# A decayed linear attention that feeds a SwiGLU block: half steps of the third tile ahead of the first outputs, and loads of group 7 ahead of a transpose

## The chip, the cores and the metric

The kernel runs on one core of a Trainium2 chip. The metric is the device time of one execution in microseconds. A core has five engines that run their own instruction streams: TensorE (PE in the profile; PEld is its weight load), VectorE (DVE), ScalarE (ACT), GpSimd (POOL) and SyncE (SP). [...] Transfers between HBM and the core's memory are issued by SP and ACT here and run on the core's 16 DMA engines.

## The reference

Inputs are q, k and v of shape (batch 4, heads 8, sequence 768, head size 64), one decay per head, lam, and three weight matrices. The first part is causal linear attention with decay, worked in blocks of 64 positions:

```
for b in range(nb):
    intra = einsum('bhic,bhjc->bhij', qb, kb) * Dmask     # lam ** (i - j), lower triangle
    intra = einsum('bhij,bhjd->bhid', intra, vb)
    inter = einsum('bhid,bhde->bhie', qb * lam_pow, kv_state)
    out[block] = intra + inter
    kv_state = lam_block * kv_state + einsum('bhsd,bhse->bhde', kb * rev_pow, vb)
```

Its result, laid out as 3072 tokens of 512 numbers, is x of the second part:

```
g = x @ w_gate                     # 512 -> 1536
silu = g * (1 / (1 + exp(-g)))
out = (silu * (x @ w_val)) @ w_out # 1536 -> 512
```

## The kernel before

**Groups and tiles.** The kernel works the sequence in blocks of 128. A group is one batch and two such blocks; there are 12 groups, 0 to 11. Two groups make a tile of 512 tokens (four blocks b of 128), so there are six tiles t, 0 to 5. Attention goes group by group, the SwiGLU block tile by tile. A tile has 12 steps fc, one for each 128 columns of the 1536. ffn_gate (L508) runs four matmuls over the input rows (L514) and Silu on ACT (L518); ffn_val (L520) runs four more (L528) and multiplies on DVE into h (L531). A full step is 512 columns wide. A half step takes two of the four blocks and is 256 wide: blocks 0 and 1 need only the attention of the tile's first group, blocks 2 and 3 only that of the second. ffn_out (L538) makes the output of one block: twelve matmuls over h and w_out (L547), a copy on ACT (L549) and a DMA that ACT issues (L550). The very last output is made in two halves of 256 columns, the second copied by DVE and sent by SP.

**A group of attention.** Its k, q and v are loaded by SP (load_fp32, L93; from group 6 on each of k and q in four DMAs, L106, v in two). cast_scaled (L255) casts k on ACT (L258) and scales q on DVE (L260) and then issues a DMA transpose on SP (L251); groups 0 to 2 are transposed on TensorE instead (pe_transpose, L289). v_scale (L235) makes v_s from v on POOL (L238). upd_mm (L366, matmuls L382) multiplies k by v_s for the running state, upd_copy (L390) copies that out on ACT (L404), and state (L410) adds it up on POOL (L421 to L432). scores (L308, matmuls L326, from group 6 on L352) multiplies q by k; the causal mask is put on by DVE later, by run_later (L333, L357). core_a (L490) multiplies q by the state (L461), core_b (L495) multiplies the masked scores by v_s (L474), and evac (L481) casts the result to xt, the input of the SwiGLU block (L486). Two helpers bundle these: ahead(g) does upd and scores; attend(g) does core_a of g, then upd_mm, upd_copy and scores of g + 1, then core_b of g and state of g + 1.

**What sets the order.** Each engine runs its instructions in the order in which the program issues them. The order is written by hand: lines 574 to 665 are a fixed start (groups 0 and 1 and the first steps), and then a list of steps with a plan of calls that follow each step (at, L675; the loop of L766 issues a step and then its calls). Tile 1 is done in 24 half steps, s1a and s1b. Behind the last of them come, in one row, the four outputs of tile 0 with the attention of group 5, the cast, transpose and v_s of group 6 and the loads of group 7 between them (L736 to L746). Tile 2 follows in twelve full steps, with ahead(6) after step 2, cast_scaled of groups 7 and 8 after steps 3 and 7, attend(6) after step 6, attend(7) after step 10, and the outputs of tile 1 after steps 0, 3, 7 and 9.

**Queues and buffers.** SP's queue carries all loads and all DMA transposes in program order; ACT's carries the outputs. PSUM is used as a ring of eight banks. w_out comes in six pieces that are cast by wo_cast, five on POOL and one on ACT. h has two tiles of 12 columns blocks each. At the very start, before any data is there, TensorE runs matmuls on constants (warm_up, L127), and in between them the matmul that spreads lam over the partitions (L163).

Of the kernel before, what the change touches and what calls it, by code (L numbers as in the profile page):

```python
# [37 lines left out]
def _body(ctx, tc, nc, q, k, v, lam, moe_w_gate, moe_w_val, moe_w_out, out):  # L38
    B, H, S, D = q.shape
    HP = H // 2  # L40
    BLK = 128
# [4 lines left out]
    FC = DFF // 128  # L46
    NG = NBLK * B // 2
# [22 lines left out]
    h_pool = ctx.enter_context(tc.tile_pool(name="h", bufs=2))  # L70
# [90 lines left out]
    lam_ps = bank()  # L161
    warm_up(4)
    nc.tensor.matmul(lam_ps[:, 0:H], ones[:, 0:128], lam_row, start=True, stop=True)  # L163
    warm_up(3)
# [355 lines left out]
    def ffn_val(t, fc, b0=0, b1=B):  # L520
        if ("h", t) not in st:
            st[("h", t)] = h_pool.tile([128, FC, B, BLK], BF16, name="h", tag="h")
        h_sb, xt, sil = st[("h", t)], st[("xt", t)], st[("sil", t, fc, b0)]
        N = (b1 - b0) * BLK
        fs = slice(fc * 128, fc * 128 + 128)
        vp = bank()
        for mc in range(MC):
            nc.tensor.matmul(vp[:, 0:N], wv_sb[:, mc, fs],  # L528
                             xt[:, b0 // 2:b1 // 2, mc].rearrange("p g b n -> p g (b n)"),
                             start=(mc == 0), stop=(mc == MC - 1))  # L530
        nc.vector.tensor_tensor(out=h_sb[:, fc, b0:b1].rearrange("p b n -> p (b n)"),  # L531
                                in0=sil[:, 0:N], in1=vp[:, 0:N], op=ALU.mult)
# [5 lines left out]
    def ffn_out(t, b, last=False):  # L538
        h_sb = st[("h", t)]
        osb = osb_pool.tile([128, DM], FP32, name="osb", tag="osb")  # L540
        row = groups[2 * t + b // 2][0] * S + (groups[2 * t + b // 2][1] * 2 + b % 2) * BLK
        halves = ((0, DM // 2, nc.scalar.copy, nc.scalar), (DM // 2, DM, nc.vector.tensor_copy, nc.sync)) \
            if last else ((0, DM, nc.scalar.copy, nc.scalar),)
        for c0, c1, fn, eng in halves:
            ps = bank()[:, 0:c1 - c0]
            for fc in range(FC):
                nc.tensor.matmul(ps, h_sb[:, fc, b], wo_sb[:, fc, c0:c1],  # L547
                                 start=(fc == 0), stop=(fc == FC - 1))
            fn(out=osb[:, c0:c1], in_=ps)  # L549
            eng.dma_start(out=bass.AP(tensor=out.tensor, offset=out.offset + row * DM + c0,  # L550
                                      ap=[[DM, 128], [1, c1 - c0]]),
                          in_=osb[:, c0:c1])
# [104 lines left out]
    w_cast()  # L657
# [29 lines left out]
    at(s0[4], load_group, 2, "v")  # L687
# [8 lines left out]
    at(s0[8], v_scale, 2, nc.gpsimd)  # L696
# [34 lines left out]
    at(s1b[6], v_scale, 5, nc.gpsimd)  # L731
    at(s1b[8], wo_cast)
    at(s1b[9], core_a, 4)
    at(s1b[10], core_b, 4)
    at(s1b[10], wo_cast, ACTC)
    at(s1b[11], ffn_out, 0, 0)  # L736
    at(s1b[11], ahead, 5)
    at(s1b[11], run_later, 3)
    at(s1b[11], ffn_out, 0, 1)
    at(s1b[11], core_a, 5)  # L740
    at(s1b[11], ffn_out, 0, 2)
    at(s1b[11], core_b, 5)
    at(s1b[11], cast_scaled, 6)
    at(s1b[11], load_group, 7)
    at(s1b[11], v_scale, 6, nc.gpsimd)
    at(s1b[11], ffn_out, 0, 3)  # L746

    outs = [(1, b) for b in range(4)]
    for t in range(2, NG // 2):
        sn = [step(t, fc) for fc in range(FC)]  # L750
        if t == 2:
            at(sn[2], ahead, 6)
        for j, g in ((3 if t == 2 else 0, 2 * t + 3), (7 if t == 2 else 6, 2 * t + 4)):
            if g < NG:
# [3 lines left out]
                at(sn[1 + j], v_scale, g, nc.gpsimd)  # L758
        if t + 1 < NG // 2:
            at(sn[6 if t == 2 else 4], attend, 2 * t + 2)  # L760
            at(sn[10], attend, 2 * t + 3)
        for n, o in zip((0, 3, 7, 9), outs):
            at(sn[n], ffn_out, *o)
# [42 lines left out]
```

## Time and profile before

| | us |
|---|---|
| runs, median of 4 (lowest to highest) | 228.44 (227.96 to 229.01) |
| the profiled execution's own time | 228.06 |
| its span, first to last instruction | 226.4 |
| busy: PE, PEld | 219.4, 118.5 |
| busy: ACT, DVE, POOL | 107.2, 90.2, 89.6 |

The busy times are shares of one span and engines overlap, so they don't add up. Matmuls are pipelined: a matmul row gives the time from the first start to the modelled end, and the next row can start before it. How long a matmul really takes in a stream is read from where the next one starts: 0.86 for four of 512 columns and 0.44 for four of 256 in the chain of work. The chain is the run of work that ended last, followed back; a wait is put down to what came last before it ended. Lines with a trailing q (SPq, ACTq) are the engine's sequencer issuing a DMA.

### The profile page before, as it was taken

The page shows a single profiled execution, that of the slowest core. Times are in us where ns is not written, and L with a number is a line of the kernel's source. Part 1 is how long each engine was busy: PE and PEld are TensorE (multiplying, and loading weights), DVE is VectorE, ACT ScalarE, POOL GpSimd, SP SyncE. Part 2 cuts the span into 40 slices and gives each one's busy share as a digit, 9 for nine tenths or more (in the row PEclk, how much of TensorE's full clock was granted, in tenths as well). Part 3 has the DMA queues.
Part 4 walks back from the last instruction along what each step waited for, and adds up shares of the span by engine and source line. Part 5 has one row for each costly group of instructions (what it writes and reads, how often), then busy time and mean ns, then how long its engine had stood idle before and what let it go on. Part 6 is the DMA issues. An engine that isn't in the chain of part 4 may idle for free.

```text
span 226.4 us, 5902 instructions
## 1 busy us (share of the span) xinstructions
PE 219.4 (97%) x2443; PEld 118.5 (52%) x2443; DVE 90.2 (40%) x151; ACT 107.2 (47%) x209; POOL 89.6 (40%) x131
## 2 busy tenths in 40 slices
PE   8889999999999999999999999999999999999994
PEld 3666455878864444454544544544544444444443
DVE  2664357685934215545253262253242123222200
ACT  6878584754663536354443453553533423322221
POOL 6676737642894403969262192191150000000000
PEclk9999999999999999999999999999999999999998
DMA  6999999899989487889867749905101101101122
GB/s 198 342 360 382 367 341 315 225 247 373 397 153 213 145 184 193 214 180 230 211 145 191 184 96 229 225 12 139 49 3 48 46 3 46 46 0 46 49 93 93
DMA packets 88012, 39.70 MB, mean 175 GB/s; under 512 B 57650, under 2 KB 83506, under 8 KB 87986
## 3 DMA queue, kind: packets, MB, share of 16 engines
q1 hardware_dynamic: 83474, 32.64, 53.8%
q10 hardware_dynamic: 4512, 6.69, 8.3%
q8 instruction: 19, 0.31, 0.6%
q14 instruction: 7, 0.06, 0.1%
HBM read 28.31 MB, written 6.29 MB: 153 GB/s over the span
## 4 chain that ended last, share of the span: by engine, by line
PE 80%; DMA 8%; POOL 6%; SPq 3%; issue 1%; ACT 0%; DVE 0%; DVEq 0%; POOLq 0%
PE bank L547 27%; PE bank L514 23%; PE bank L528 23%; DMA v<-in_v_dram 5%; DMA wraw<-in_moe_w_val_dram 3%; POOL v_s L238 3%; SPq L99 2%; PE bank L474 2%; PE bank L461 2%; PE bank L382 2%; POOL wo_sb L232 1%; POOL kvf L421 1%; PE bank L352 1%; POOL kvs L424 1%; PE bank L326 1%
## 5 line engine op out<-in xcount | busy, mean ns | idle before, releaser
L531 DVE TENSOR_TENSOR h<-sil,bank 128x512 bf16<-128x512 bf16 (+1 forms) x87 | 51.5, 595 | 108.0 <-PE bank L528 94.1
L514 PE MATMUL bank<-xt,wg_sb 128*128 128x512 bf16 (+1 forms) x348 | 76.6, 343 | 0.0
L528 PE MATMUL bank<-xt,wv_sb 128*128 128x512 bf16 (+1 forms) x348 | 76.4, 342 | 0.0
L518 ACT ACTIVATE sil<-bank 128x512 bf16<-128x512 f32 (+1 forms) x87 | 45.9, 527 | 44.4 <-PE bank L514 41.4
L547 PE MATMUL bank<-wo_sb,h 128*128 128x512 bf16 (+1 forms) x300 | 65.8, 371 | 0.4 <-POOL wo_sb L232 0.4
L528 PEld LDWEIGHTS <-wv_sb 128*128 128x128 bf16 x348 | 34.0, 98 | 28.3 <-POOL wv_sb L221 0.2
L514 PEld LDWEIGHTS <-wg_sb 128*128 128x128 bf16 x348 | 32.4, 98 | 27.2 <-DVE xt L486 0.3
L547 PEld LDWEIGHTS <-h 128*128 128x128 bf16 x300 | 29.1, 98 | 33.0 <-issue 0.7
L549 ACT COPY osb<-bank 128x512 f32<-128x512 f32 (+1 forms) x24 | 13.8, 576 | 53.3 <-PE bank L547 51.3
L238 POOL TENSOR_TENSOR v_s<-v,dec 128x1024 bf16<-128x1024 f32 (+1 forms) x14 | 23.2, 1665 | 11.7 <-DMA v<-in_v_dram 5.9
L421 POOL TENSOR_TENSOR kvf<-kvs,ups 128x256 f32<-128x256 f32 x8 | 5.8, 726 | 46.2 <-ACT ups L404 40.6
L333 DVE TENSOR_TENSOR ssb<-bank,causal 128x512 bf16<-128x512 f32 x24 | 15.3, 684 | 3.6 <-PE bank L326 3.5
L486 ACT CAST xt<-bank 128x512 bf16<-128x512 f32 x21 | 12.8, 667 | 2.9 <-PE bank L474 2.4
L430 POOL CAST kvn<-kvf 64x256 bf16<-64x256 f32 x24 | 12.5, 519 | 1.5
L421 POOL TENSOR_TENSOR kvf<-kvf,ups 128x256 f32<-128x256 f32 x16 | 12.7, 792 | 0.6
L404 ACT COPY ups<-bank 128x256 f32<-128x256 f32 (+1 forms) x24 | 9.5, 449 | 2.5 <-PE bank L382 1.5
L258 ACT CAST qk<-kraw 128x1024 bf16<-128x1024 f32 x9 | 9.4, 1040 | 0.9 <-DMA kraw<-in_k_dram 0.9
L260 DVE TENSOR_TENSOR qk<-qraw,qdn 128x1024 bf16<-128x1024 f32 x6 | 7.9, 1314 | 4.2 <-DMA qraw<-in_q_dram 4.1
L357 DVE TENSOR_TENSOR ssb<-bank,causaln 128x512 bf16<-128x512 f32 x12 | 8.3, 688 | 1.2 <-PE bank L352 1.1
L221 POOL CAST wv_sb<-wraw 128x1024 bf16<-128x1024 f32 (+1 forms) x6 | 5.8, 968 | 5.3 <-DMA wraw<-in_moe_w_val_dram 5.2
L232 POOL CAST wo_sb<-woraw 128x1024 bf16<-128x1024 f32 x5 | 5.8, 1181 | 4.6 <-DMA woraw<-in_moe_w_out_dram 4.6
L474 PE MATMUL bank<-ssb,v_s 64*64 64x128 bf16 (+1 forms) x384 | 6.8, 208 | 0.5 <-ACT guard L445 0.5
(63 smaller groups left out, 118.3 us busy)
## 6 DMA issues: line engine op xcount, KB each, us to landing
out_dram<-osb ACTq DMA_DIRECT2D x23, 256.0 KB, 2.1
v<-in_v_dram SPq DMA_DIRECT2D x16, 256.0 KB, 4.5
woraw<-in_moe_w_out_dram SPq DMA_DIRECT2D x6, 512.0 KB, 7.5
kraw<-in_k_dram SPq DMA_DIRECT2D x24, 128.0 KB, 3.3
qraw<-in_q_dram SPq DMA_DIRECT2D x24, 128.0 KB, 3.5
wraw<-in_moe_w_gate_dram SPq DMA_DIRECT2D x5, 512.0 KB, 7.3
wraw<-in_moe_w_val_dram SPq DMA_DIRECT2D x5, 512.0 KB, 6.9
kraw<-in_k_dram SPq DMA_DIRECT2D x4, 512.0 KB, 6.8
```

Source lines behind the costliest of these rows:

```text
L238: eng.tensor_tensor(out=st[("vs", g)][:, h0:h1], in0=st[("v", g)][:, h0:h1].rearrange("p h (s d) -> p h s d", s=2), in1=vfac(g, h0, h1), o ...
L333: nc.vector.tensor_tensor(out=ssb[:, h2, 2 * c:2 * c + 2].rearrange("p a s n -> p a (s n)"), in0=sp[(c, h2)].rearrange("p (a x) -> p a x", ...
L421: nc.gpsimd.tensor_tensor(out=o, in0=f, in1=u, op=ALU.add)
L430: nc.gpsimd.tensor_copy(out=o[64 - h2 * 64:128 - h2 * 64], in_=f[h2 * 64:h2 * 64 + 64])
L474: nc.tensor.matmul(op[r][h2 * 64:h2 * 64 + 64, cols(g, hp, s)], v_s[ps, 2 * hp + h2, s], ssb[ps, h2, hp * 2 + s] if g >= NAT0 else ssb[ps, ...
L486: fns[r](out=xt[:, g % 2, :, r].rearrange("p h (m s) -> p h s m", s=2) if g < NAT0 else xt[:, g % 2, :, :, r * M:r * M + M], in_=op[r].rea ...
L514: nc.tensor.matmul(gp[:, 0:N], wg_sb[:, mc, fs], xt[:, b0 // 2:b1 // 2, mc].rearrange("p g b n -> p g (b n)"), start=(mc == 0), stop=(mc = ...
L518: nc.scalar.activation(sil[:, 0:N], gp[:, 0:N], AF.Silu)
L528: nc.tensor.matmul(vp[:, 0:N], wv_sb[:, mc, fs], xt[:, b0 // 2:b1 // 2, mc].rearrange("p g b n -> p g (b n)"), start=(mc == 0), stop=(mc = ...
L531: nc.vector.tensor_tensor(out=h_sb[:, fc, b0:b1].rearrange("p b n -> p (b n)"), in0=sil[:, 0:N], in1=vp[:, 0:N], op=ALU.mult)
L547: nc.tensor.matmul(ps, h_sb[:, fc, b], wo_sb[:, fc, c0:c1], start=(fc == 0), stop=(fc == FC - 1))
L549: fn(out=osb[:, c0:c1], in_=ps)
```

## The change

It has these parts.

- **Half steps.** Four half steps of tile 2 (fc 0 to 3, blocks 0 and 1) are put behind tile 1 and ahead of the four outputs of tile 0; in tile 2 itself steps 0 to 3 are then half steps for blocks 2 and 3. h becomes half tiles of six column blocks, five of them instead of two whole ones. group 4's result is cast to xt by DVE and ACT, not by ACT alone.
- **Group 7.** Its k and q are loaded ahead of the first output of tile 0, and so ahead of group 6's transpose on SP; its v behind that transpose. Its v_scale is issued ahead of ahead(6), and so ahead of the state of group 6 on POOL.
- **Order in tile 2.** ahead(6) goes from step 2 to step 4, cast_scaled of groups 7 and 8 from steps 3 and 7 to 4 and 8, attend(6) from step 6 to step 7; the outputs of tile 1 follow steps 1, 5, 7 and 9. v_scale of group 5 goes behind the fifth cast of w_out.
- **Halves for group 2 and for one weight.** v of group 2 is loaded and scaled in two halves, and POOL casts one piece of w_val in two halves.
- **Start and end.** Ahead of lam's matmul stand thirty matmuls of 64 rows and 8 columns, in alternating halves of the rows, and two of 512 columns, instead of four of 512; behind it stand four instead of three. The last output is split into 384 columns (ACT) and 128 (DVE and SP).

```diff
--- before.py
+++ after.py
@@ -44,6 +44,7 @@
     DFF = moe_w_gate.shape[1]
     MC = DM // 128
     FC = DFF // 128
+    FH = FC // 2
     NG = NBLK * B // 2
     M = BLK // 2
 
@@ -67,7 +68,7 @@
     vs_pool = ctx.enter_context(tc.tile_pool(name="vs", bufs=4))
     ssb_pool = ctx.enter_context(tc.tile_pool(name="ssb", bufs=2))
     xt_pool = ctx.enter_context(tc.tile_pool(name="xt", bufs=2))
-    h_pool = ctx.enter_context(tc.tile_pool(name="h", bufs=2))
+    h_pool = ctx.enter_context(tc.tile_pool(name="h", bufs=5))
     sil_pool = ctx.enter_context(tc.tile_pool(name="sil", bufs=3))
     osb_pool = ctx.enter_context(tc.tile_pool(name="osb", bufs=3))
     kv_pool = ctx.enter_context(tc.tile_pool(name="kv", bufs=1))
@@ -159,9 +160,13 @@
            for b in range(B)]
 
     lam_ps = bank()
+    b = bank()
+    for n in range(30):
+        r = slice(n % 2 * 64, n % 2 * 64 + 64)
+        nc.tensor.matmul(b[r, 0:8], warm[r, 0:64], warm[r, 0:8], start=True, stop=True, skip_group_check=True)
+    warm_up(2)
+    nc.tensor.matmul(lam_ps[:, 0:H], ones[:, 0:128], lam_row, start=True, stop=True)
     warm_up(4)
-    nc.tensor.matmul(lam_ps[:, 0:H], ones[:, 0:128], lam_row, start=True, stop=True)
-    warm_up(3)
     def warm_into(b, n, cols=256):
         for _ in range(n):
             nc.tensor.matmul(b[:, 0:cols], warm[:, 0:128], warm[:, 0:cols], start=True, stop=True)
@@ -518,9 +523,10 @@
         nc.scalar.activation(sil[:, 0:N], gp[:, 0:N], AF.Silu)
 
     def ffn_val(t, fc, b0=0, b1=B):
-        if ("h", t) not in st:
-            st[("h", t)] = h_pool.tile([128, FC, B, BLK], BF16, name="h", tag="h")
-        h_sb, xt, sil = st[("h", t)], st[("xt", t)], st[("sil", t, fc, b0)]
+        hn = ("h", t, fc // FH)
+        if hn not in st:
+            st[hn] = h_pool.tile([128, FH, B, BLK], BF16, name="h", tag="h")
+        h_sb, xt, sil = st[hn], st[("xt", t)], st[("sil", t, fc, b0)]
         N = (b1 - b0) * BLK
         fs = slice(fc * 128, fc * 128 + 128)
         vp = bank()
@@ -528,7 +534,7 @@
             nc.tensor.matmul(vp[:, 0:N], wv_sb[:, mc, fs],
                              xt[:, b0 // 2:b1 // 2, mc].rearrange("p g b n -> p g (b n)"),
                              start=(mc == 0), stop=(mc == MC - 1))
-        nc.vector.tensor_tensor(out=h_sb[:, fc, b0:b1].rearrange("p b n -> p (b n)"),
+        nc.vector.tensor_tensor(out=h_sb[:, fc % FH, b0:b1].rearrange("p b n -> p (b n)"),
                                 in0=sil[:, 0:N], in1=vp[:, 0:N], op=ALU.mult)
 
     def ffn_fc(t, fc, b0=0, b1=B):
@@ -536,15 +542,14 @@
         ffn_val(t, fc, b0, b1)
 
     def ffn_out(t, b, last=False):
-        h_sb = st[("h", t)]
         osb = osb_pool.tile([128, DM], FP32, name="osb", tag="osb")
         row = groups[2 * t + b // 2][0] * S + (groups[2 * t + b // 2][1] * 2 + b % 2) * BLK
-        halves = ((0, DM // 2, nc.scalar.copy, nc.scalar), (DM // 2, DM, nc.vector.tensor_copy, nc.sync)) \
+        halves = ((0, DM - 128, nc.scalar.copy, nc.scalar), (DM - 128, DM, nc.vector.tensor_copy, nc.sync)) \
             if last else ((0, DM, nc.scalar.copy, nc.scalar),)
         for c0, c1, fn, eng in halves:
             ps = bank()[:, 0:c1 - c0]
             for fc in range(FC):
-                nc.tensor.matmul(ps, h_sb[:, fc, b], wo_sb[:, fc, c0:c1],
+                nc.tensor.matmul(ps, st[("h", t, fc // FH)][:, fc % FH, b], wo_sb[:, fc, c0:c1],
                                  start=(fc == 0), stop=(fc == FC - 1))
             fn(out=osb[:, c0:c1], in_=ps)
             eng.dma_start(out=bass.AP(tensor=out.tensor, offset=out.offset + row * DM + c0,
@@ -654,7 +659,10 @@
     ffn_gate(0, 1, 0, 2)
     ffn_gate(0, 0, 2, 4)
     w_piece(6, 8)
-    w_cast()
+    w_cast((ACTC,))
+    wv2, wv2r = w_raw.pop(0)
+    for c in range(2):
+        POOLC(out=wv2[:, :, c * 128:c * 128 + 128], in_=wv2r[:, :, c * 128:c * 128 + 128])
     ring[0] = 4
     ffn_val(0, 0, 2, 4)
     ffn_val(0, 1, 0, 2)
@@ -684,7 +692,8 @@
     at(s0[3], swapped_q_table)
     at(s0[4], w_cast)
     at(s0[4], state, 1)
-    at(s0[4], load_group, 2, "v")
+    at(s0[4], load_fp32, 2, nc.sync, v, "v", 0, H // 2)
+    at(s0[4], load_fp32, 2, nc.sync, v, "v", H // 2, H)
     at(s0[5], load_group, 3)
     at(s0[6], w_cast)
     at(s0[7], load_group, 4, "kq")
@@ -693,7 +702,8 @@
     at(s0[8], pe_transpose, 2, 0)
     at(s0[8], pe_transpose, 2, 1)
     at(s0[8], w_cast)
-    at(s0[8], v_scale, 2, nc.gpsimd)
+    at(s0[8], v_scale, 2, nc.gpsimd, 0, H // 2)
+    at(s0[8], v_scale, 2, nc.gpsimd, H // 2, H)
     at(s0[9], scores, 2)
     at(s0[9], run_later, 4)
     at(s0[10], upd_mm, 2)
@@ -728,38 +738,43 @@
     at(s1b[6], run_later, 2)
     at(s1b[6], wo_cast)
     at(s1b[6], wo_cast)
-    at(s1b[6], v_scale, 5, nc.gpsimd)
     at(s1b[8], wo_cast)
+    at(s1b[8], v_scale, 5, nc.gpsimd)
     at(s1b[9], core_a, 4)
-    at(s1b[10], core_b, 4)
+    at(s1b[10], core_b, 4, SPLIT)
     at(s1b[10], wo_cast, ACTC)
-    at(s1b[11], ffn_out, 0, 0)
-    at(s1b[11], ahead, 5)
-    at(s1b[11], run_later, 3)
-    at(s1b[11], ffn_out, 0, 1)
-    at(s1b[11], core_a, 5)
-    at(s1b[11], ffn_out, 0, 2)
-    at(s1b[11], core_b, 5)
-    at(s1b[11], cast_scaled, 6)
-    at(s1b[11], load_group, 7)
-    at(s1b[11], v_scale, 6, nc.gpsimd)
-    at(s1b[11], ffn_out, 0, 3)
+    NH = 4
+    s2 = [step(2, fc, 0, 2) for fc in range(NH)][-1]
+    at(s2, load_group, 7, "kq")
+    at(s2, ffn_out, 0, 0)
+    at(s2, ahead, 5)
+    at(s2, run_later, 3)
+    at(s2, ffn_out, 0, 1)
+    at(s2, core_a, 5)
+    at(s2, ffn_out, 0, 2)
+    at(s2, core_b, 5)
+    at(s2, cast_scaled, 6)
+    at(s2, load_group, 7, "v")
+    at(s2, v_scale, 6, nc.gpsimd)
+    at(s2, ffn_out, 0, 3)
 
     outs = [(1, b) for b in range(4)]
     for t in range(2, NG // 2):
-        sn = [step(t, fc) for fc in range(FC)]
+        sn = [step(t, fc, 2 if t == 2 and fc < NH else 0) for fc in range(FC)]
         if t == 2:
-            at(sn[2], ahead, 6)
-        for j, g in ((3 if t == 2 else 0, 2 * t + 3), (7 if t == 2 else 6, 2 * t + 4)):
+            at(sn[4], v_scale, 7, nc.gpsimd)
+            at(sn[4], ahead, 6)
+        for j, g in ((4 if t == 2 else 0, 2 * t + 3), (8 if t == 2 else 6, 2 * t + 4)):
             if g < NG:
                 at(sn[j], cast_scaled, g)
                 if g + 1 < NG:
                     at(sn[j], load_group, g + 1)
-                at(sn[1 + j], v_scale, g, nc.gpsimd)
+                if g > 7:
+                    at(sn[1 + j], v_scale, g, nc.gpsimd)
         if t + 1 < NG // 2:
-            at(sn[6 if t == 2 else 4], attend, 2 * t + 2)
+            at(sn[7 if t == 2 else 4], attend, 2 * t + 2)
             at(sn[10], attend, 2 * t + 3)
-        for n, o in zip((0, 3, 7, 9), outs):
+        for n, o in zip((1, 5, 7, 9) if t == 2 else (0, 3, 7, 9), outs):
             at(sn[n], ffn_out, *o)
         outs = [(t, b) for b in range(4)]
```

## The prediction

> **What bounds the kernel now.** I read the page's head and engine shares, then its chain of work, then the waits of TensorE, and last the timeline wherever TensorE stood still.
>
> ```profile
> span 226.4 us, 5902 instructions
> PE 219.4 (97%) x2443; PEld 118.5 (52%) x2443; DVE 90.2 (40%) x151; ACT 107.2 (47%) x209; POOL 89.6 (40%) x131
> PE 80%; DMA 8%; POOL 6%; SPq 3%; issue 1%; ACT 0%; DVE 0%; DVEq 0%; POOLq 0%
> ```
>
> TensorE (PE) is busy 97% of the span and holds 80% of the chain; the next engine has 47%. A part of this change can pay only where PE waits, or in the first 15 us and the last 4 us. The timeline shows these places.
>
> ```profile
> 4.42 0.63 PE L289 MATMUL bank<-ident,qk 128*128 128x128 bf16 x4
> 4.68 0.62 ACT L273 CAST qk<-kraw 128x512 bf16<-128x512 f32 x1
> 5.35 0.61 PE L289 MATMUL bank<-ident,qk 128*128 128x128 bf16 x4
> 5.75 0.85 PE L167 MATMUL bank<-const-bfloat16-1.0 128*128 128x256 bf16 x3
> 6.63 0.45 PE L326 MATMUL bank<-qkt 64*64 64x128 bf16 x16
> 7.47 0.49 PE L167 MATMUL bank<-const-bfloat16-1.0 128*128 128x256 bf16 x3
> ...
> 34.83 1.91 POOL L238 TENSOR_TENSOR v_s<-v,dec 128x1024 bf16<-128x1024 f32 x1 [0.48 <-DMA v<-in_v_dram]
> 35.69 1.03 PE L528 MATMUL bank<-xt,wv_sb 128*128 128x512 bf16 x4
> 36.80 0.45 PE L382 MATMUL bank<-v_s,qk 64*64 64x64 bf16 x32
> ...
> 65.97 1.89 PE L547 MATMUL bank<-wo_sb,h 128*128 128x512 bf16 x8
> 67.20 1.04 POOL L232 CAST wo_sb<-woraw 128x1024 bf16<-128x1024 f32 x1
> 68.29 1.02 PE L547 MATMUL bank<-wo_sb,h 128*128 128x512 bf16 x4 [0.42 <-POOL wo_sb L232]
> ```
>
> Three 256-wide matmuls take 0.85 at 5.75 and 0.49 at 7.47: TensorE runs at about half rate until some 6.7 us. At 35.69 four matmuls of 0.216 (0.86 for four in the chain) stream until 36.55; the next starts at 36.80, because v_s of group 2 is ready at 36.74. About 0.09 is the usual price of going over to small matmuls (the same change at 86.11 + 0.86 = 86.97 to 87.06), so the wait is 0.15. At 65.97 eight matmuls end their streaming at 67.70 and the ninth starts at 68.29, after the last piece of w_out is cast: a wait of 0.59, the longest of PE after 15 us.
>
> **Half steps ahead of the first outputs.** Four half steps (L514 and L528, 256 wide) now stand between 65.97 and ffn_out(0, 0). Four 256-wide matmuls take 0.44 in the chain, so a half step is 0.87 and the first output starts at 65.97 + 3.5 = 69.5. v_scale of group 5 (1.91) also leaves the place ahead of the fifth cast of w_out, so POOL ends that at 65.38 + 1.04 = 66.4, and ACT its own piece near 66.9. The 0.59 goes, with 2.6 of cover. v_s of group 5 is then ready at 66.4 + 1.91 = 68.3 and wanted after the first output, at 72.1. Price: two halves (1.746) against a full step (1.727), four times, **+0.08**. The first half step reads group 4's xt. L486 on ACT twice took 1.33 (65.21 to 66.54); shared between DVE (0.73) and ACT (0.67) it ends near 65.95, so PE loses perhaps **+0.05**. ACT's cast of w_out then delays Silu of the last half step of tile 1 to about 66.9, where that bank is wanted again only at 68.6. h has five half tiles, so the new h writes onto no tile that an output still reads. Sum: -0.59 + 0.08 + 0.05 = **-0.46**.
>
> **Loads of group 7.** Eight k and q issues (0.65 each) now stand ahead of group 6's transpose on SP. SP is free at 71.5, so they are issued by about 77; group 6's casts come near 82 (79.4 in the trace, and PE is 2.9 later), and the transpose doesn't wait on SP. [...] scores(6) wants it near 90.3. I take **0**, with 2 of slack. v_scale of group 7 now precedes state(6) on POOL: group 7's v is issued near 85, lands near 89, is scaled by 91, and state(6), whose input leaves ACT near 91, hardly waits. Its last operand was ready 5.4 after its start (88.27 to 93.66), so at 96.7; core_a(6) wants it at 98.4. Also 0.
>
> **The order of tile 2.** cast_scaled(8) moves from step 7 to step 8 while scores(8) stays after step 10. These rows price it.
>
> ```profile
> 103.53 1.23 DVE L260 TENSOR_TENSOR qk<-qraw,qdn 128x1024 bf16<-128x1024 f32 x1 [1.35 <-DMA qraw<-in_q_dram]
> 103.94 1.03 PE L528 MATMUL bank<-xt,wv_sb 128*128 128x512 bf16 x4
> 104.89 1.87 SPq L251 DMA_TRANSPOSE qkt<-qk  x1
> 105.07 0.69 DVE L531 TENSOR_TENSOR h<-sil,bank 128x512 bf16<-128x512 bf16 x1 [0.31 <-PE bank L528]
> 111.45 0.48 PE L352 MATMUL bank<-qkt 64*64 64x64 bf16 x30
> ```
>
> From step 8's L528 (103.94) PE needs 7.45 to reach scores(8) (111.4); that order stays. The new chain from the same point: 1.13 to h on DVE, h 0.69, the second mask of group 7 0.68 (L357 at 101.50), q cast 1.31 (mean of its group), transpose 3.93 from issue to landing (104.89 to 108.82), less about 0.1 of overlap: 7.7, and 0.05 to wake PE. The transpose is late by about **+0.3**; from 0 (shortest cast and landing) to 0.9 (a cast of 1.75 beside POOL, as at 91.19). In the old order that cover was 2.6. The loads of group 9 behind it on SP slip by about 2.3 and still end 2.5 ahead of scores(9).
>
> **v of group 2 in halves.** Two loads and two scales: POOL starts the first half at 34.35, when its cast ends, and ends both by 34.35 + 2 x 1.05 = 36.45. **-0.15**. The extra issue on SP (0.7) is hidden, since its DMA engines are full there (1.07 of a share). Splitting POOL's cast of w_val (L221, ready at 20.14, used at 20.31) changes nothing unless PE arrives earlier: 0.
>
> **The start.** Thirty 64-row matmuls of 8 columns and two 512-wide take the place of four 512-wide ahead of lam; behind lam stand four, not three (0.43 each). No row shows the tiny ones. Low end: L382 at 36.80, 32 in 0.38, 12 ns each, 0.36 in all. High end: half-rate transposes, 107 ns each (4.42 to 4.85 for four), 3.2. Nearest is L326 at 6.63, 16 in 0.38, 24 ns, 0.72. [...] I take 0.8. Then lam comes as before (two 512-wide were 0.85), q's transposes come 0.4 later, and k's at 5.28 + 0.21 = 5.49, not 5.35. Ahead of k's stood ACT's cast, ended at 5.29, so only **+0.14** shows; it passes through ACT, scores and the masks of DVE to 14.55, for which PE waits at 14.71. Could they lift the clock earlier? [...] The trace can't check that: it shows one rise between 6.4 and 7.5. By its rows, a full rate at 5.35 would save four transposes of 0.05 and some 0.1 of scores, -0.3. [...]
>
> **The end.**
>
> ```profile
> 223.06 0.43 DVE L549 COPY osb<-bank 128x256 f32<-128x256 f32 x1 [9.69 <-DMA out_dram<-osb]
> 223.51 0.38 SPq L550 DMA_DIRECT2D out_dram<-osb  x1
> ```
>
> Matmul columns stay the same. DVE copies 128 columns: 0.69 at 512 and 0.42 at 256 make 0.29 at 128, -0.13. The last DMA carries 64 KB: 2.1 at 256 KB and 1.8 at 128 KB make about 1.65, -0.12. ACT's 384 columns land some 0.2 earlier than that. **-0.25**.
>
> **Sum.** -0.46 + 0.3 - 0.15 + 0.14 - 0.25 = -0.42. The profiled execution took 228.06 (span 226.4) and would take 227.6; it lies 0.38 under the median of the runs, so 228.44 - 0.42 = **228.0**.
>
> **Rivals.**
> Early clock and no late transpose (0.22): PE stands at 14.71 for a chain that passes through half-rate work, which speaks for it; the free-running window against. Sum -0.46 - 0.15 - 0.25 - 0.3 = -1.16, 227.3 or less.
> The tiny matmuls are dear (0.12), the rival on the slow side: one after another, not in pairs. Place: ahead of lam. [...]
> Group 8's transpose is very late (0.08): the nine transposes of the trace take 3.7 to 8.2 from issue to landing, median 4.0 (the view of L251). At 6 the stall is 2.4, 230.1. Against it: group 8's loads are down by 106.1.
> The w_out wait goes but another takes its place at the same spot (0.08): group 4's xt or a bank held by a late Silu, some 0.5; 228.5.
> The likeliest (0.50): 227.5 to 228.5.
>
> **The numbers.** About 0.5% (1.14) is what can be told from no change: faster is under 227.3, slower over 229.6. Faster: most of the first rival and an edge of the likeliest, 0.22. Slower: half of the dear matmuls and nearly all of the late transpose, 0.14. The rest, 0.64. Range 227.0 to 229.5: it takes in the first rival and the 53 ns case, and leaves out the two far ends.
>
> **What would show it.** No PE wait on w_out; half steps from 66 to 69.5; a gap ahead of L352 of group 8 near 111; L382 of group 2 without its 0.15; k's first transposes near 5.5; a last copy of 128 columns near 0.29. Wrong would be: k's transposes after 6, a gap at scores(6), or full rate before 5.

## The result, and the profile after

The changed kernel takes **227.89 us** (median of 44 runs, 226.84 to 229.51), the kernel before 228.63 beside it (63 runs). The ratio, taken round by round, is 0.9983, interval [0.997, 0.9995]: a gain of 0.39 us (0.0017 x 228.6; the two medians stand 0.74 apart). It is clear of 1, but inside the 0.5% that was called no change.

The profiled execution took 229.39, with a span of 227.6, 1.5 above its kernel's median; the one of before took 228.06, with 226.4. So the two pages, laid side by side, would say "1.3 slower". The first lines of the page of after, and its chain:

```profile
span 227.6 us, 6044 instructions
PE 220.7 (97%) x2504; PEld 122.4 (54%) x2504; DVE 90.7 (40%) x156; ACT 107.2 (47%) x212; POOL 89.9 (39%) x133
PE 91%; SPq 3%; DMA 3%; DVE 1%; POOL 0%; issue 0%; ACT 0%; DVEq 0%
```

TensorE now holds 91% of the chain, not 80%: DMA and POOL are gone from it in mid-kernel. To see where time came and went I took the start of the same instruction in several traces, in us from the start of the span. The third column is the profiled execution of after, the fourth the same kernel profiled again, the fifth the changed kernel with the start of before (both are runs of the next section). In brackets: later (+) or earlier (-) than before.

| first instruction of | before | after | after, again | after, old start |
|---|---|---|---|---|
| q's first transposes | 4.42 | 4.91 (+0.49) | 4.91 (+0.50) | 4.42 (0.00) |
| k's first transposes | 5.35 | 5.37 (+0.02) | 5.55 (+0.21) | 5.24 (-0.10) |
| first full gate step | 19.45 | 21.25 (+1.80) | 19.36 (-0.09) | 19.45 (0.00) |
| upd_mm of group 2 | 36.80 | 38.45 (+1.65) | 37.06 (+0.26) | 36.65 (-0.15) |
| core_b of group 4 | 64.52 | 66.45 (+1.93) | 65.39 (+0.87) | 64.37 (-0.15) |
| ffn_out(0, 0) | 65.97 | 71.47 (+5.49) | 70.41 (+4.43) | 69.39 (+3.41) |
| upd_mm of group 5 | 69.24 | 74.15 (+4.91) | 73.09 (+3.85) | 72.07 (+2.83) |
| ffn_out(1, 2) | 100.48 | 101.94 (+1.46) | 101.05 (+0.56) | 99.89 (-0.59) |
| ffn_out(2, 0) | 115.72 | 117.27 (+1.54) | 116.33 (+0.60) | 115.19 (-0.54) |
| last matmul | 222.69 | 224.28 (+1.59) | 223.35 (+0.65) | 222.21 (-0.48) |
| end | 226.35 | 227.65 (+1.29) | 226.71 (+0.36) | 225.59 (-0.76) |

Between ffn_out(0, 0) and ffn_out(1, 2) the four half steps are given back: four full steps of before are half steps there, which is why +3.41 turns into -0.59.

**What spoilt the profiled execution.** 1.80 of its loss lies ahead of the first full step. The timeline of after there:

```profile
0.84 0.96 PE L166 MATMUL bank<-const-bfloat16-1.0 64*64 64x8 bf16 x30 [0.84 <-PEq L805]
4.91 0.51 PE L294 MATMUL bank<-ident,qk 128*128 128x128 bf16 x4
5.37 0.39 PE L294 MATMUL bank<-ident,qk 128*128 128x128 bf16 x4
...
13.47 1.05 POOL L243 TENSOR_TENSOR v_s<-v,dec 128x512 bf16<-128x512 f32 x1 [1.06 <-DMA v<-in_v_dram]
14.57 0.38 PE L387 MATMUL bank<-v_s,qk 64*64 64x64 bf16 x24 [0.71 <-POOL v_s L243]
```

The second half of group 1's v landed at 13.40 (12.25 in the trace of before). POOL waited 1.06 for it and PE 0.71 for POOL. That moved core_b of group 1 by 0.30 (15.21 against 14.91). The other 1.50 is the clock. In the windows view (columns: window, its length, busy time of PE, PEld, DVE, ACT and POOL with their instructions, granted clock of PE, DMA share, GB/s), cut so that the half-rate stretch stands alone:

```profile
8.58:11.99 3.41, 3.13 (x110) 2.37 (x104) 2.45 (x6) 2.89 (x6) 2.87 (x5) 1.00 1.15 346
11.99:15.40 3.41, 2.21 (x72) 1.48 (x75) 2.43 (x6) 2.47 (x6) 2.35 (x4) 1.00 1.14 344
15.40:18.81 3.41, 3.41 (x50) 2.23 (x43) 0.78 (x2) 1.27 (x3) 1.45 (x3) 0.50 0.98 334
```

PE was busy 2.21 of the 3.41 us before 15.40, and then ran the next 3.41 us at half rate. Of the 44 runs 5 have such a stretch by their mean granted clock (0.991 or 0.992 instead of 0.998 to 1.0), and these took 229.19 to 229.51. Five more took 229.10 to 229.41 at full clock, so the clock is not the only thing that makes the upper end. The second trace of the same kernel has no half-rate stretch.

**The places that the prediction named.** First w_out, in the profiled execution of after (timeline):

```profile
66.64 3.01 POOL L237 CAST wo_sb<-woraw 128x1024 bf16<-128x1024 f32 x3
67.97 0.61 PE L519 MATMUL bank<-xt,wg_sb 128*128 128x256 bf16 x4
...
69.61 1.92 POOL L243 TENSOR_TENSOR v_s<-v,dec 128x1024 bf16<-128x1024 f32 x1
71.03 0.60 PE L534 MATMUL bank<-xt,wv_sb 128*128 128x256 bf16 x4
71.47 2.75 PE L552 MATMUL bank<-wo_sb,h 128*128 128x512 bf16 x12
```

The twelve matmuls of ffn_out(0, 0) are one row now, with no wait. Before they were eight, a wait on wo_sb, and four. POOL's casts end at 69.65, 1.8 ahead of the output. The end of the kernel, same view:

```profile
224.60 0.29 DVE L554 COPY osb<-bank 128x128 f32<-128x128 f32 x1 [9.69 <-DMA out_dram<-osb]
224.91 0.37 SPq L555 DMA_DIRECT2D out_dram<-osb  x1
```

The last copy took 0.29 where 0.43 stood.

### The profile page after: what moved, and what is told of

Its sections match the earlier page's. It is cut to its first block, busy times and chain, and to the rows that moved or that the text cites. A ratio compares the mean times of both kernels' runs of the same rounds, so it can differ in the third digit from the quotient of the medians.

```text
span 227.6 us, 6044 instructions
## 1 busy us (share of the span) xinstructions
PE 220.7 (97%) x2504; PEld 122.4 (54%) x2504; DVE 90.7 (40%) x156; ACT 107.2 (47%) x212; POOL 89.9 (39%) x133
## 4 chain that ended last, share of the span: by engine, by line
PE 91%; SPq 3%; DMA 3%; DVE 1%; POOL 0%; issue 0%; ACT 0%; DVEq 0%
PE bank L519 28%; PE bank L552 28%; PE bank L534 27%; DMA v<-in_v_dram 3%; SPq L100 3%; PE bank L479 2%; PE bank L466 2%; PE bank L387 2%; DVE ssb L338 1%; PE bank L357 1%; PE bank L331 1%; POOL v_s L243 0%; PE bank L294 0%; DVE h L537 0%; SPq L114 0%
## 5 line engine op out<-in xcount | busy, mean ns | idle before, releaser
L519 PE MATMUL bank<-xt,wg_sb 128*128 128x512 bf16 (+1 forms) x364 | 77.8, 337 | 0.0
L534 PE MATMUL bank<-xt,wv_sb 128*128 128x512 bf16 (+1 forms) x364 | 77.5, 336 | 0.0
L552 PE MATMUL bank<-wo_sb,h 128*128 128x512 bf16 (+2 forms) x300 | 65.7, 371 | 0.0
L534 PEld LDWEIGHTS <-wv_sb 128*128 128x128 bf16 x364 | 35.7, 98 | 27.0 <-issue 0.2
L519 PEld LDWEIGHTS <-wg_sb 128*128 128x128 bf16 x364 | 34.2, 99 | 26.6 <-DVE xt L491 0.5
L552 PEld LDWEIGHTS <-h 128*128 128x128 bf16 x300 | 28.6, 98 | 32.5
L491 ACT CAST xt<-bank 128x512 bf16<-128x512 f32 x20 | 12.2, 661 | 3.0 <-PE bank L479 2.4
L426 POOL TENSOR_TENSOR kvf<-kvf,ups 128x256 f32<-128x256 f32 x16 | 11.6, 726 | 0.6
L237 POOL CAST wo_sb<-woraw 128x1024 bf16<-128x1024 f32 x5 | 5.1, 1042 | 6.5 <-DMA woraw<-in_moe_w_out_dram 6.5
L479 PEld LDWEIGHTS <-v_s 64*64 64x64 bf16 x384 | 5.6, 108 | 2.0 <-issue 2.0
```

Source lines behind the costliest of these rows:

```text
L426: nc.gpsimd.tensor_tensor(out=o, in0=f, in1=u, op=ALU.add)
L479: nc.tensor.matmul(op[r][h2 * 64:h2 * 64 + 64, cols(g, hp, s)], v_s[ps, 2 * hp + h2, s], ssb[ps, h2, hp * 2 + s] if g >= NAT0 else ssb[ps, ...
L491: fns[r](out=xt[:, g % 2, :, r].rearrange("p h (m s) -> p h s m", s=2) if g < NAT0 else xt[:, g % 2, :, :, r * M:r * M + M], in_=op[r].rea ...
L519: nc.tensor.matmul(gp[:, 0:N], wg_sb[:, mc, fs], xt[:, b0 // 2:b1 // 2, mc].rearrange("p g b n -> p g (b n)"), start=(mc == 0), stop=(mc = ...
L534: nc.tensor.matmul(vp[:, 0:N], wv_sb[:, mc, fs], xt[:, b0 // 2:b1 // 2, mc].rearrange("p g b n -> p g (b n)"), start=(mc == 0), stop=(mc = ...
L552: nc.tensor.matmul(ps, st[("h", t, fc // FH)][:, fc % FH, b], wo_sb[:, fc, c0:c1], start=(fc == 0), stop=(fc == FC - 1))
```

## The experiments

Ratios are to the kernel before, run beside each on the same chip (medians there 228.81, 228.63 and 228.5). Every kernel computes the whole result.

### Old start in the changed kernel

```diff
-    b = bank()
-    for n in range(30):
-        ...
-    warm_up(2)
-    nc.tensor.matmul(lam_ps[:, 0:H], ones[:, 0:128], lam_row, start=True, stop=True)
     warm_up(4)
+    nc.tensor.matmul(lam_ps[:, 0:H], ones[:, 0:128], lam_row, start=True, stop=True)
+    warm_up(3)
```

> The changed kernel with the start of before: four constant matmuls of 512 columns, lam, three more, and no tiny ones. Theory: outside the first 20 us the change is worth about -0.8 (in the two traces -0.58 at w_out, -0.15 at group 2, -0.25 at the end, +0.2 for half steps, xt and the late transpose), and the start is neutral apart from when the clock rises and falls, which depends on the execution. Then this kernel does as the changed one, a ratio of 0.998 to the kernel before, and now and then loses about 1.7 in the first 20 us as the changed kernel did in its trace. Rival: the new start itself loses about 0.4 on average, since PE does less there; then this kernel reaches the -0.8, a ratio of 0.9965.

It took 227.78 (227.35 to 229.66, 22 runs), 0.9961 [0.9943, 0.998]. The changed kernel and this one were run once more, side by side:

> The changed kernel unaltered, beside the same kernel with the old start on one chip. So far the ratios were 0.9983 (changed) and 0.9961 (changed with the old start), from different calls. Theory: the new start costs 0.3 to 0.5 (q's first transposes come 0.43 to 0.49 later in every trace with it, k's 0.1 to 0.2 when the clock isn't full by then), so this kernel is 0.9975 to 0.999. Rival: the difference was between calls, and both kernels come out within 0.1% of each other.

> The changed kernel with the start of before, again. Theory: 0.9955 to 0.997, and 0.3 to 0.5 under the changed kernel in the same call. Rival: the same as the changed kernel.

The changed kernel took 227.88, 0.9972 [0.9953, 0.9991]; with the old start 227.55, 0.9965 [0.9943, 0.9986]. The old start comes out lower both times: 0.5 us between the ratios taken apart (0.9961 against 0.9983), and side by side 0.2 by the ratios and 0.3 by the medians, with intervals that overlap. The trace of the last one, 227.30 in all, has no half-rate stretch and no late landing of weight, so it is the clean comparison with before: the table's fifth column, -0.76 at the end.

The first trace with the old start showed something else. Its timeline, at the transpose of group 6 and at scores(6):

```profile
82.22 4.62 SPq L252 DMA_TRANSPOSE qkt<-qk  x1
89.95 0.45 PE L383 MATMUL bank<-v_s,qk 64*64 64x64 bf16 x32
91.67 0.45 PE L353 MATMUL bank<-qkt 64*64 64x64 bf16 x32 [1.27 <-DMA qkt<-qk]
...
93.91 1.91 POOL L239 TENSOR_TENSOR v_s<-v,dec 128x1024 bf16<-128x1024 f32 x1 [12.88 <-DMA v<-in_v_dram]
100.33 0.21 PE L462 MATMUL bank<-qkt,kvn 64*64 64x64 bf16 x1 [0.15 <-POOL kvn L431]
```

And the trace of the repeat, in which nothing waits:

```profile
82.21 2.09 SPq L252 DMA_TRANSPOSE qkt<-qk  x1
...
89.17 1.92 POOL L239 TENSOR_TENSOR v_s<-v,dec 128x1024 bf16<-128x1024 f32 x1 [9.72 <-PE bank L515]
91.14 0.73 POOL L422 TENSOR_TENSOR kvf<-kvs,ups 128x256 f32<-128x256 f32 x1
```

In before, with no load of group 7 ahead of it, the same transpose held SP 1.69:

```profile
79.38 1.69 SPq L251 DMA_TRANSPOSE qkt<-qk  x1
```

Twice the same kernel, the same moment of issue: once the transpose landed 9.4 after it and PE stood 1.27, once 5.1 after it, in time. Of seven traces with k and q of group 7 ahead of this transpose, two waited for it; they are the two in which the issue held SP for over 4 us (4.62 and 4.01). The v of group 7 differs as much: its scale on POOL starts at 93.91 in the one trace and at 89.17 in the other. (That last row names PE, but v's second half landed at 89.0, just ahead of it.) In the first the state of group 6, behind that scale, is late for core_a of group 6: from there to upd_mm of group 7 PE needs 0.62, and 0.27 in the second.

### The new start alone

```diff
-    warm_up(4)
+    b = bank()
+    for n in range(30):
+        ...
+    warm_up(2)
     nc.tensor.matmul(lam_ps[:, 0:H], ones[:, 0:128], lam_row, start=True, stop=True)
-    warm_up(3)
+    warm_up(4)
```

> The kernel before with only the new start (thirty tiny matmuls, two of 512 columns, lam, four of 512). Theory: within 0.15 of the kernel before (ratio 0.9993 to 1.0007), lam 0.06 later, k's first transposes not more than 0.14 later. Rival: +0.4, a ratio of 1.0018.

> The kernel before with only the new start, once more, for a second trace and a second comparison. The first comparison gave 1.0037 [1.0013, 1.0061], against the theory that the start is neutral; its trace came from one of the quickest executions and shows nothing of the loss. If the loss is real, the ratio is again 1.002 to 1.006, and this trace shows where it sits: the clock released a window later, a long wait on v_s of group 1, or a longer wait on w_out. If it was chance, the ratio is 0.999 to 1.001.

229.81, 1.0037 [1.0013, 1.0061], and 230.19, 1.0061 [1.0031, 1.009]: slower by 1.0 and 1.6 us, far more than the +0.14 of the sum and more than in the changed kernel. But the start itself doesn't show it. The second trace reaches its first steps 0.27 later, and waits 1.71 at the output of tile 0 (timeline):

```profile
67.03 1.91 POOL L242 TENSOR_TENSOR v_s<-v,dec 128x1024 bf16<-128x1024 f32 x1
68.88 1.04 POOL L236 CAST wo_sb<-woraw 128x1024 bf16<-128x1024 f32 x1
69.97 1.02 PE L551 MATMUL bank<-wo_sb,h 128*128 128x512 bf16 x4 [1.71 <-POOL wo_sb L236]
```

w_out's last two pieces landed at 65.2 and 66.5, not at 62.5 and 63.8, and the scale of group 5's v stands ahead of the last cast. That cast ends at 69.92, 1.68 later than in before, and upd_mm of group 5 starts 1.69 later.

Why w_out is late in this trace can be followed one step back on SP. In before, and then in this trace, the transpose of group 4 and the issue of w_out's six pieces:

```profile
45.79 1.63 SPq L251 DMA_TRANSPOSE qkt<-qk  x1
50.77 4.14 SPq L227 DMA_DIRECT2D woraw<-in_moe_w_out_dram  x6
```

```profile
46.19 3.59 SPq L255 DMA_TRANSPOSE qkt<-qk  x1
52.47 5.47 SPq L231 DMA_DIRECT2D woraw<-in_moe_w_out_dram  x6
```

The transpose held SP 2.0 longer, and w_out was issued 1.7 later. In four of the five traces with the whole new start it held SP 3.5 to 4.2, in the eight with the old start 1.6 to 2.3. What makes it hold longer was not found. It is not all of it either: with the old start, too, the last piece landed at 66.0 to 66.7 in four traces.

To see whether it is the tiny matmuls or the fourth matmul behind lam, only the latter:

```diff
     nc.tensor.matmul(lam_ps[:, 0:H], ones[:, 0:128], lam_row, start=True, stop=True)
-    warm_up(3)
+    warm_up(4)
```

> The kernel before with four constant matmuls of 512 columns, lam, and four (not three) more: the new start without its tiny matmuls. Theory A (the tiny matmuls count too little as work for the clock, so that it is released a window later in more executions): no loss here, ratio 0.999 to 1.001. Theory B (the fourth matmul behind lam delays k's first transposes by up to 0.2 and with them everything): the same loss as with the whole new start, 1.002 to 1.006.

229.11 (227.85 to 231.31, 11 runs), 1.0009 [0.9976, 1.0042]. It lies between the two and excludes neither. Its trace waits 1.5 on w_out as well. This settles nothing.

### Half steps, loads and order of tile 2 alone

The kernel before with the half steps, the h half tiles, the order of tile 2, the loads of group 7, the scale of group 5 and the split evac; start, end, v of group 2 and w_val as before.

```diff
+    NH = 4
+    s2 = [step(2, fc, 0, 2) for fc in range(NH)][-1]
+    at(s2, load_group, 7, "kq")
...
+            at(sn[4], v_scale, 7, nc.gpsimd)
+            at(sn[4], ahead, 6)
```

> The kernel before with the half steps, the order of tile 2, the loads of group 7, the move of the scale of group 5's v and the shared cast of group 4 alone: old start, old end, v of group 2 in one piece, one cast of that w_val piece. Theory: -0.59 + 0.08 + 0.05 + 0.1 to 0.3 (the late transpose of group 8) = -0.4 to -0.2, a ratio of 0.998 to 0.999; no wait of PE on w_out, a wait of 0.15 left ahead of L382 of group 2. Rival (another wait takes the place): a ratio of 1.000.

227.97 (227.58 to 230.26), 0.9981 [0.9957, 1.0005]. The w_out wait is gone, and PE waits 0.2 on v_s of group 2, which the change's halves would have removed. The v of group 7 was late as well (scaled from 92.48), and core_a of group 6 took 0.3 longer. The point estimate is that of the whole change.

### Only the scale of group 5's v behind the fifth cast

```diff
-    at(s1b[6], v_scale, 5, nc.gpsimd)
     at(s1b[8], wo_cast)
+    at(s1b[8], v_scale, 5, nc.gpsimd)
```

> The kernel before with only the scale of group 5's v moved behind the fifth cast of w_out on POOL. Theory: the cast ends 1.9 earlier (66.3), before PE wants it (67.7), so the wait of 0.59 goes without any half step, -0.5 to -0.6, ratio 0.9975; v_s of group 5 is then ready at 68.3, just ahead of its use at 68.6. Rival (the half steps are what removes it, because the last piece of w_out lands or ACT casts it too late): the wait stays at 0.3 or more, ratio 0.9985 to 1.000.

228.29, 0.9984 [0.9961, 1.0007]. In its trace w_out was late as well, and no output waits. But this is where the wait went:

```profile
61.61 1.04 POOL L232 CAST wo_sb<-woraw 128x1024 bf16<-128x1024 f32 x1 [2.33 <-DMA woraw<-in_moe_w_out_dram]
63.85 0.24 PE L461 MATMUL bank<-qkt,kvn 64*64 64x128 bf16 x1 [0.80 <-POOL kvn L432]
...
68.54 1.91 POOL L238 TENSOR_TENSOR v_s<-v,dec 128x1024 bf16<-128x1024 f32 x1
70.50 0.45 PE L382 MATMUL bank<-v_s,qk 64*64 64x64 bf16 x32 [0.85 <-POOL v_s L238]
```

POOL stands 2.33 for a piece of w_out. Behind that cast waits the state of group 4, which core_a(4) wants (0.80), and the scale that was moved is late for upd_mm of group 5 (0.85). In this execution the move alone passes the wait on, and the half steps would give the time in which both fit. The runs don't separate the two: 0.9984 here and 0.9981 with the half steps, with intervals that nearly coincide. That the move alone is enough where w_out lands early stays possible. The wait of core_a(4) is in the changed kernel too: between upd_mm(2) and core_b(4) its two traces lose 0.28 and 0.61, the one with w_out in time nothing.

### Loads of group 7 behind the transpose again

From the changed kernel with the old start.

```diff
-    at(s2, load_group, 7, "kq")
     at(s2, ffn_out, 0, 0)
...
     at(s2, cast_scaled, 6)
-    at(s2, load_group, 7, "v")
+    at(s2, load_group, 7)
```

> The changed kernel with the start of before, and with k and q of group 7 loaded behind group 6's transpose again, as before the change. The trace of the same kernel with the loads ahead showed the transpose issued over 4.6 and landed at 91.6, with 1.3 of wait of PE on it. Theory (the loads ahead delay the transpose in some executions): no such wait here in any execution, the upper runs (above 228.5) are fewer, the median the same or up to 0.2 lower, ratio to the kernel before 0.995 to 0.9965. Rival (the loads ahead are needed, since group 7's casts then come too late): a wait at scores(7), +0.3 or more.

234.78 (233.94 to 235.84, 6 runs), 1.0283 [1.0252, 1.0313]: 7 us for what the sum carried as 0. Timeline, and then the windows view (columns as above):

```profile
90.57 1.28 SPq L107 DMA_DIRECT2D v<-in_v_dram  x2
...
96.81 1.91 POOL L239 TENSOR_TENSOR v_s<-v,dec 128x1024 bf16<-128x1024 f32 x1 [16.86 <-DMA v<-in_v_dram]
98.69 0.72 POOL L422 TENSOR_TENSOR kvf<-kvs,ups 128x256 f32<-128x256 f32 x1
99.92 0.21 PE L462 MATMUL bank<-qkt,kvn 64*64 64x64 bf16 x1 [1.48 <-POOL kvn L431]
```

```profile
97.68:101.10 3.42, 1.19 (x7) 0.41 (x5) 1.10 (x2) 0.39 (x1) 3.22 (x5) 1.00 1.00 227
101.10:104.51 3.41, 1.80 (x99) 1.53 (x103) 0.00 (x0) 0.36 (x2) 3.06 (x7) 0.50 0.81 182
104.51:107.93 3.42, 3.09 (x48) 1.48 (x41) 0.69 (x1) 1.86 (x4) 3.09 (x7) 0.50 0.90 205
```

The v of group 7, last in SP's queue, lands near 96.8. Its scale stands on POOL ahead of the state of group 6, so POOL is idle 16.86 and the state starts at 98.69, about when core_a(6) wants its result. PE waits 5.8 in all (3.8 for kvn, the state that core_a reads, and 2.0 for the transpose of group 8), and the clock falls to half for 6.83. All six runs have it (mean granted clock 0.985).

### The scale of group 7's v behind the state

From the changed kernel with the old start, the other half of the pair.

```diff
         if t == 2:
-            at(sn[4], v_scale, 7, nc.gpsimd)
             at(sn[4], ahead, 6)
+            at(sn[4], v_scale, 7, nc.gpsimd)
```

> The changed kernel with the old start, and the scale of group 7's v behind the state of group 6 on POOL again, as in the order of before; the loads stay ahead. With the other order but late loads PE waited for the state (ratio 1.028). Theory: the state of group 6 takes POOL 7.3 and now ends near 98.5, the scale 1.9 more, and the state matmuls of group 7 want it at about 99.0, so PE waits about 1.4 on v_s there: ratio about 1.002, 1.4 above the changed kernel with the old start. Rival: POOL is quicker or PE later, and there is no wait, 0.996.

228.94 (228.61 to 230.89, 14 runs), 1.0009 [0.9985, 1.0033], 1.4 over the old-start kernel beside it.

```profile
98.45 1.91 POOL L239 TENSOR_TENSOR v_s<-v,dec 128x1024 bf16<-128x1024 f32 x1
100.42 0.45 PE L383 MATMUL bank<-v_s,qk 64*64 64x64 bf16 x32 [0.85 <-POOL v_s L239]
```

Behind the state the scale ends at 100.36 and upd_mm(7) waits 0.85. (This trace also waits 0.5 for the transpose of group 6, as the old-start kernel did in one of its two traces.) So the place ahead of the state is worth about 1, if v is there; the place of the loads is what makes v be there.

### Filling TensorE ahead of the clock's fall

```diff
-    warm_into(up[0], 1)
+    warm_into(up[0], 3)
...
-    warm_into(st[("op", 1)][0], 2)
+    warm_into(st[("op", 1)][0], 4)
```

> The changed kernel with two more constant matmuls of 256 columns ahead of the state matmuls of group 1 and two more behind them (0.11 each at full rate), in places where PE stands still in both traces (13.4 to 14.6). Theory: the fall of the clock to half rate at 15.40 in the trace of the changed kernel came from PE standing still between 12.0 and 15.4; with more work there it falls in fewer executions, so the median is the same or up to 0.3 lower than the changed kernel's and the runs above 229 are fewer. Rival: the fall has nothing to do with the idle time and the four matmuls only cost up to 0.4.

228.08 (227.4 to 230.53), 0.9974 [0.995, 0.9998]: not to be told from the changed kernel. In its trace group 1's v was late again (PE waited 0.93) and the clock stayed full. Later, behind the place where it fell in after, stands this:

```profile
21.58 0.60 PE L519 MATMUL bank<-xt,wg_sb 128*128 128x512 bf16 x2 [1.08 <-ACT wg_sb L226]
```

A late weight cost 1.08 there. One of its 22 runs still has a half-rate stretch by its mean clock (0.993, 230.53). Whether the filling helps is open.

### Group 6's transpose earlier

If the late transpose of group 6 makes the upper end of the times, an earlier issue should take it away. From the changed kernel with the old start: cast and transpose of group 6 ahead of the third output, with only k of group 7 ahead of it in SP's queue.

```diff
-    at(s2, load_group, 7, "kq")
+    at(s2, load_group, 7, "k")
...
     at(s2, core_a, 5)
+    at(s2, cast_scaled, 6)
+    at(s2, load_group, 7, "q")
     at(s2, ffn_out, 0, 2)
     at(s2, core_b, 5)
-    at(s2, cast_scaled, 6)
```

> The changed kernel with the old start, and group 6's cast and transpose ahead of the third output instead of behind it, with k of group 7 loaded ahead of the transpose and q behind it. Theory: the transpose is issued near 80.5, lands by 85 in place of 88 to 91.6, so scores(6) (wanted near 90) never waits; group 7's q and v come 2 later than in the changed kernel, v by 90, in time for the scale ahead of the state. Median equal to or 0.1 to 0.3 below the changed kernel with the old start, ratio 0.995 to 0.9965. Rival: ACT's cast or DVE's wait for q of group 6 delays group 5's result, or v of group 7 lands so late that POOL is held up: +0.5 or more.

227.48 (227.01 to 228.22, 19 runs), 0.995 [0.9933, 0.9967]: the lowest of all, and no run over 228.22 where the old-start kernel beside it had 229.71. Its price is in the trace:

```profile
79.98 3.07 SPq L252 DMA_TRANSPOSE qkt<-qk  x1
92.73 1.91 POOL L239 TENSOR_TENSOR v_s<-v,dec 128x1024 bf16<-128x1024 f32 x1 [11.39 <-DMA v<-in_v_dram]
99.16 0.21 PE L462 MATMUL bank<-qkt,kvn 64*64 64x64 bf16 x1 [0.24 <-POOL kvn L431]
```

v of group 7 is scaled 3.6 later (92.73 against 89.17), and core_a(6) waits for the state: it is 0.88 from there to upd_mm(7), not 0.27. This kernel beats the kernel before; against the changed kernel (0.9972) and the old-start kernel (0.9965), both run beside it, the intervals overlap.

## Why the prediction was right, point by point

The forecast was 228.0, the sum -0.42; measured were 227.89 and -0.39 by the ratio. Most terms are borne out one by one in the clean trace (changed kernel, old start); the total is in part the balance of two wrong ones.

- **w_out and the half steps, -0.46: right.** The half steps took 3.50 where 3.5 was forecast, with 0.07 at group 4's xt (forecast 0.05). At the wait all three traces of the table that have them gain 0.58, and once the half steps are given back the net is -0.44 (from -0.15 to -0.59). But the 0.59 taken from the trace of before is one execution's number: kernels without half steps waited 0.6 to 1.7 in four traces, and no trace with them waited at the output. The term grew with how late w_out landed (0.59 with the last piece at 63.8 in before, 1.71 with it at 66.5 in the second trace with the new start alone). That it takes the half steps, and not the moved scale alone, rests on one trace.
- **Loads of group 7, "0, with 2 of slack": the size of the slack was wrong.** The slack came from a landing near 88, the casts near 82 and the one transpose of the trace of before (79.38 to 84.99, 5.6 from issue to landing). It lasted 9.4 in one execution, with a wait of 1.27. In two of seven traces PE waited for it (1.27 and 0.48); in the others the transpose was in time, as forecast. The earlier issue, with half of the loads ahead, had no such wait and no upper tail. That fits a transpose that the loads ahead delay, but so does the longer hold of SP's queue in the two (4.62 and 4.01, against 2.09 in the repeat), and no run separates them.
- **Scale of group 7's v, "also 0": right in three of six traces.** Scaled by 91 was forecast, 91.1 measured in the clean trace. In the other five with this order the scale starts at 90.7 to 94.8, and in the three where it starts after 92 core_a of group 6 takes 0.3 longer, for the state: the landing near 89 was forecast without a spread. What I had not priced either was the cover: with the loads behind the transpose it costs about 7, behind the state 1.4.
- **Late transpose of group 8, +0.3: right in kind, too large.** It was issued at 107.31, and from ffn_out(1, 2) to ffn_out(2, 0) the clean trace loses 0.05, the two of the changed kernel 0.08 and 0.04, with no wait on a DMA at scores(8).
- **v of group 2 in halves, -0.15: right** in two of three traces (+1.80 to +1.65, 0.00 to -0.15). In the second of the changed kernel PE lost 0.35 there instead, 0.2 of it waiting for POOL's cast ahead of a transpose of group 2. And the trace with only group 5's scale moved, without halves, had v 0.2 earlier and upd_mm of group 2 at 36.67 as well: the term hangs on one landing.
- **The start, +0.14: the term that was wrong in size, and its cause is only partly known.** The tiny matmuls span 0.84 to 1.74 with the step to the next, 0.9 where 0.8 was taken; no run shows the 0.8, nor the 53 ns apiece that the range takes in: measured is 30 ns each (0.9 for thirty, in after). Then q's transposes came 0.49 later and k's at 5.37 and 5.55 (5.49 forecast). So far the chain was right. The start costs the changed kernel 0.2 to 0.5 (not settled), and the kernel before 1.0 to 1.6 by the medians, where the traced loss is at w_out. One step of that was followed, the transpose of group 4 that holds SP longer; its cause was not found.
- **The clock, for which the sum took nothing: right.** First full rate came at 5.1 to 7.0 after the span's start in the eight traces with the old start, at 5.1 to 8.0 in the five with the new one. The window that speaks against the first rival was a premise of mine, not a reading of before; what the traces show is that in after the rise at 5.16 and the fall at 15.40 are 10.24 apart, three times the 3.41 of half rate behind it. But with the new start the rise may come later: in the first trace with it alone PE was busy all the time from 1.16 to 4.57, the tiny matmuls 0.58 of it, and full rate came only at 7.99. Whether the tiny ones count for less was not tested.
- **The end, -0.25: right.** -0.30 and -0.28 between last matmul and end, the copy 0.29 as worked out.

So the clean trace gains 0.76 without the start (-0.44 - 0.15 + 0.05 - 0.28, and 0.06 lost in tiles 2 to 5), where the sum had -0.56 without it (the 0.3 for group 8 was 0.05). About half of it is missing in the median of the changed kernel. The new start and executions with a late transpose, a late state of group 4 or 6 or a fallen clock are seen to cost time; how the missing 0.37 divides among them was not measured. That the sum of -0.42 came so near to the -0.39 is luck in part: an error of +0.25 at group 8 stands against missing terms of the same size.

## What to carry to other kernels

A wait that ends with a transfer had no one length here (group 6's transpose landed 5.1 and 9.4 after the same moment of issue): take it from several executions, and credit independent work put in front of it with the longest of them. When two calls are moved together (a load forward, and the work on it ahead of other work on the same engine: POOL here, idle 16.86 with the state behind a scale that waited), price each as if the other were absent; that shows what cover the pair rests on (7 us and 1.4 here). And before two profiles are compared, place both among the runs of their kernels: here the one of the quicker kernel lay 1.5 us above its median and would have turned the sign.

## What was not expected of the hardware

- **TensorE's clock fell in mid-kernel without a long pause, and busy time alone didn't say when.** In after it fell with single waits of at most 0.71; the window 11.99 to 15.40 ahead of it held only 2.21 of busy time, and one with 1.19 lost the clock too. But windows with 2.24 and 2.25 at the same place (11.97 to 15.38 and 12.06 to 15.47, two other traces) kept the full rate, and so did windows with less: 2.00 in the run with late loads (118.16 to 121.57), 1.89 at the wait on w_out in the trace with four matmuls behind lam, and 1.70 at that wait in the second trace with the new start alone, whose row (columns as above) is

```profile
67.21:70.62 3.41, 1.70 (x9) 0.68 (x7) 0.42 (x1) 0.92 (x2) 2.71 (x2) 1.00 0.76 172
```

  PE's work in that window is nine matmuls, all 512 wide; the window of after holds none of that width. Whether the kind of work decides was not tested. In after the stretches of one granted clock last 10.24, 3.41 and 208.21, in before the one at full rate 218.45: 3, 1, 61 and 64 times 3.413, counted from the first full rate at 5.16 in after and at 6.74 in before. Against such steps, the same wait may fall into one window or be shared by two: in before the waits near 13 to 15 lay in two windows with 3.16 and 2.87.
- **Landings differed by microseconds between executions.** In two executions of the changed kernel group 1's second half of v landed at 12.22 and 13.40. In two of the changed kernel with the old start the last piece of w_out landed at 63.9 and 66.0, and one transpose held SP 2.09 and 4.62 us at the same moment of issue.
